# Retention and a routed expert layer: masks of whole chunks behind the routing's steps, the guess one place on, the second list's rows behind the list

## Chip, cores and metric

One NeuronCore of one Trainium2 chip. The metric is the device time of one execution in microseconds (us), the median of the runs shown. TensorE is called PE (PEld for its weight loads), VectorE DVE, ScalarE ACT, GpSimd POOL, SyncE SP.

## What is computed

A decaying linear attention over 4 x 768 tokens with 8 heads of 64 features, whose output rows are then routed, each to one of 8 experts:

```python
for t in range(S):
    state = gamma * state + outer(k[t], v[t])
    y[t] = scale * q[t] @ state
x = y.transpose(0, 2, 1, 3).reshape(3072, 512)
logits = x @ w_gate + modality_bias[modality_id]
e_idx = argmax(logits)                       # one expert for each token
gate_w = softmax(logits)[e_idx]
for e in range(8):
    h = maximum(x[e_idx == e] @ w1[e], 0)    # 512 -> 1024
    out[e_idx == e] = gate_w * (h @ w2[e])   # 1024 -> 512
```

## The kernel before, in words

**Retention.** The 3072 tokens are 24 chunks of 128, six for each sequence, three chunks being a routing group. `retention` (L1097) is a generator over the chunks n. The first nine (`WHOLE`) are done as whole chunks: `whole_state` (L287) adds a chunk to the state, `whole_scores(n + 1)` (L272) makes the next chunk's scores with PE (`sc`, two PSUM banks) and masks them on DVE in two steps (L283, tile `a`), `whole_out` (L303) multiplies masked scores and state into `y`, which ACT copies to `yT`. `tokens_out` (L368) turns a chunk's `yT` into token rows and logits: PE `x` (L375), DVE `lh` and half of `xs` (L383), ACT the other half of `xs` (L397), DVE the reduction to `lg` (L404). From chunk 9 on the chunks are done in halves: `scores`, `masked` (L210, the mask at L212), `heads_out`, `grown`, driven by `quarters` (L339). `hand_over` (L325) passes the state from the one form to the other at chunk 8. `decay_v` (L1020) scales the values on POOL (`vd`, L1024), two chunks ahead.

**Places.** Each `yield` of `retention` is a place. While the whole chunks run, the loop in `everything` (L1154) goes from place to place, three for each chunk (two for chunk 6), and at each runs one step of a queue `todo` (`tick`, L1032). Later, in `run_job` (L983), a job has 16 places t = 0 to 15; every odd one runs one step of `todo`, and every third runs a stretch of retention.

**Routing.** When the three chunks of a group have their logits, `route(gr)` (L1036) appends the group's steps to `todo`: `a` (L1040: bias, maximum, exponential), `a1` (one-hot choice `eq`, `mn`, `oh`, counts `cnt`, and for listed groups `crep`), `b` (`ranks` with PE `pc` at L615 and DVE `size`, `key`, `dg`; `route_b` with PE `rk`; `gates`), `c` (`rows_out` in some groups; `early_a` with PE `pk` at L637 and DVE `gt`, `rank`, `ohs` for listed groups), `d` (`early_b`: PE `pt` at L688 and DVE `lst`). `rows_out` has POOL scatter the group's three chunks of rows to `x_dram` (L481). `wait` is an empty step. The listed groups (`EVENTS`) are 1, 2, 4, 5 and 6: each puts two full slots of 256 tokens of one expert on a list, and so starts two expert jobs; group 7 lists the rest. `guess_a` (L649) guesses from group 0's counts which expert group 1 will list (PE `totg` at L651, DVE `key_g` to `lst_g`); SP reads the guess and loads that expert's weights, `raw`, 8 x 512 KB (L774).

**From the list to the first job.** When list 1 is there, SP reads it, loads the two halves of the slot's rows, `xg` (L806), which waits for the rows of groups 0 and 1, and issues the weights' loads again under the condition that the expert is not the guessed one (L776). Six places later (`AHEAD`) the jobs start; four and three places before that the first two pieces of the weights are cut into a high and a low part (`cut`, L778: ACT `hi_e` at L780, DVE `lo_e` at L782), two places before PE transposes the rows (`xp_e`, L825). A job is 8 pieces of `first_slot` (`h_e`, L840) and two halves of `second` (`o_e`, L855), whose result ACT scales (L867) and POOL scatters to the output (L868).

**What sets the order.** PE, ACT, DVE and SP run their instructions in the order in which the program text issues them (`manual_schedule`, L1209); POOL's order is set by a scheduler that follows the text where it can. Each engine works its queue in order, so a step that waits holds all behind it on that engine.

Of the kernel before, what the change touches and what calls it, by code (L numbers as in the profile page):

```python
# [29 lines left out]
EVENTS = {1: -1, 2: 1, 4: -1, 5: 1, 6: -1}  # L30
# [9 lines left out]
WHOLE = 9  # L40
# [13 lines left out]
def kernel(  # L54
# [23 lines left out]
    def bank(name):  # L78
        return ps.tile([P, 512], F32, tag="bank", name=name)
# [65 lines left out]
    def setup_a():  # L145
        nc.vector.tensor_copy(wgt[:, :, :P], ident.unsqueeze(1).to_broadcast([P, NG, P]))
        nc.vector.memset(ones, 1.0)
        nc.vector.memset(cnt[0], 0.0)
# [44 lines left out]
    att, psc, sts, vds = {}, {}, {}, {}  # L193
    pst = {}

    def rows(i):
        return slice(i * D, (i + 1) * D)

    def feat(n, i):
        return kqs[n][:, i].rearrange("p (g t) -> p g t", g=NG)  # L200
# [9 lines left out]
    def masked(n):  # L210
        att[n] = wk.tile([P, 2, NG, D], F32, tag="a", name=f"a_{n}")
        nc.vector.tensor_tensor(  # L212
            att[n].rearrange("p u g t -> p (u g) t"),
            psc.pop(n).rearrange("p u g t -> p (u g) t"),
            half.unsqueeze(1).to_broadcast([P, H, D]), op=ALU.mult,
        )
# [41 lines left out]
    def keep_state(n, u):  # L258

        s = sts[n, u] = wk.tile([P, NG, D], F32, tag="s", name=f"s{u}_{n}", bufs=3)  # L260
        b = (n - 1 + u) // NCH
        nc.scalar.copy(s, pst.pop(b) if u and n % NCH == NCH - 1 else pst[b])  # L262
# [9 lines left out]
    def whole_scores(n):  # L272
        kt, qt = feat(n, 0), feat(n, 1)
        p = [bank(f"sc{j}_{n}").rearrange("p (g t) -> p g t", g=NG) for j in range(2)]
        for g in range(NG):
            for j in range(2):
                nc.tensor.matmul(
                    p[j][:, g], kt[rows(j), g], qt[rows(j), g], start=True, stop=True,
                    skip_group_check=True,
                )  # L280
        att[n] = me.tile([P, 2, NG, P], F32, tag=f"hi1{2 + n % 2}", name=f"a_{n}")
        for j in range(2):
            nc.vector.tensor_tensor(  # L283
                att[n][:, j], p[j], mask.unsqueeze(1).to_broadcast([P, NG, P]), op=ALU.mult
            )
# [39 lines left out]
    def hand_over(n):  # L325
        old = sts.pop((n, 0))
        b = (n - 1) // NCH
        p = pst[b] = bank(f"st_{n}")[:, : NG * D].rearrange("p (g e) -> p g e", g=NG)
        for j in range(2):
            for g in range(NG):  # L330
                nc.tensor.matmul(
                    p[rows(1 - g % 2), 2 * j + g // 2], ident[:, rows(j)], old[:, g],
                    start=(j == 0 and g < 2), stop=True, skip_group_check=True,
                )
        keep_state(n, 0)
# [272 lines left out]
    def spread(counts):  # L608
        crep = mid["crep"] = passing("crep", [P, NE, SPE], BF16)
        nc.vector.tensor_copy(crep, counts.unsqueeze(2).to_broadcast([P, NE, SPE]))  # L610

    def ranks(t, which, first=None):
        crep = mid.pop("crep")
        pc = bank(f"pc{t}")
        nc.tensor.matmul(  # L615
            pc[:NCAND, 0:1], crep.rearrange("p e i -> p (e i)"), ones[:, 0:1],
            start=True, stop=True,
        )
        size = passing("size", [NCAND, 1])
        nc.vector.tensor_scalar(size, pc[:NCAND, 0:1], off_c, 0.0, op0=ALU.subtract, op1=ALU.max)  # L620
        nc.vector.tensor_scalar(
            size, size, float(SLOT), mid["keep"], op0=ALU.min, op1=ALU.mult
        )
        key = passing("key", [NCAND, 1])
        nc.vector.scalar_tensor_tensor(
            key, size, float(P), id_c, op0=ALU.mult, op1=ALU.add if which > 0 else ALU.subtract
        )
        if first is not None:
            nc.vector.tensor_tensor(key, key, first, op=ALU.add)
        dg = passing("dg", [NCAND, NCAND])  # L630
        nc.vector.tensor_scalar(dg, ident[:NCAND, :NCAND], key, None, op0=ALU.mult)
        mid["rk"] = (t, size, key, dg)
# [387 lines left out]
    def decay_v(n):  # L1020
        vv = kvs[n][:, 1].rearrange("p (h e) -> p h e", h=H)
        by = decw if n < WHOLE else dec
        vds[n] = wk.tile([P, H, D], F32, tag="vd", name=f"vd_{n}", bufs=3)
        ins = nc.gpsimd.tensor_tensor(  # L1024
            vds[n], vv, by[:, n % NCH].unsqueeze(2).to_broadcast([P, H, D]), op=ALU.mult
        )
        vd_last[:] = [getattr(ins, "ins", ins)]


    todo = []  # L1030
# [5 lines left out]
    def route(gr):  # L1036
        last = gr == NGRP - 1
        listed = gr in EVENTS or last

        def a():  # L1040
            route_a(gr, 0)

        def a1():
            route_a(gr, 1)
            route_a(gr, 2)
            if listed:
                spread(cnt[gr + 1])

        def b():
            if listed:  # L1050
                ranks(gr, EVENTS.get(gr, 1), mid["first"] if gr == min(EVENTS) else None)
            route_b(gr)
            gates(gr)

        def rows_out():
            for i in range(GRP):
                scatter(gr, i)

        def c():
            if gr not in (4, 5, 6):  # L1060
                rows_out()
            if gr == 0:
                guess_b()
            elif gr in EVENTS:
                early_a(gr)
            elif last:
                final_a()

        def d():
            early_b(gr)  # L1070

        def wait():
            pass

        if gr == min(EVENTS):

            a()
            todo.extend([a1, b, c, d])
        elif gr == 0:
            a()  # L1080
            todo.extend([a1, guess_a, b, c])
        elif gr < 5:
            todo.extend([a, a1, b, c])
            if gr in EVENTS:
                todo.append(d)
            if gr == 4:
                todo.append(rows_out)
        else:

            todo.extend([a, a1, wait, b, wait, c])  # L1090
            if gr in EVENTS:
                todo.extend([wait, d, rows_out])
            if last:
                todo.extend([wait, final_m, wait, final_b, pad_a, wait, pad_b, wait])
                todo.extend([lambda e=e: pad_c(e) for e in range(NE)])

    def retention(modi):  # L1097
        whole_scores(0)
        decay_v(1)
        setup_a()  # L1100
        prev = None
        for n in range(NN):
            if n < WHOLE:
                if (n + 1) % NCH:
                    whole_state(n)

                load_kv(n + 7 if n < 3 else n + 3)
                listed = n == (min(EVENTS) + 1) * GRP
                if listed:

                    tokens_out(*prev)
                    route(min(EVENTS))
                if n + 1 < WHOLE:
                    whole_scores(n + 1)
                else:
                    run(scores(n + 1))
                    masked(n + 1)
                    if (n + 1) % NCH:
                        hand_over(n + 1)
                yield n  # L1120
                if prev is not None and not listed:
                    tokens_out(*prev)
                    if n % GRP == 0:
                        route(n // GRP - 1)
                if n + 1 == WHOLE:
                    run(grown(n + 1, 0))
                    keep_state(n + 1, 1)
                if not listed:
                    yield n
                prev = None  # L1130
                yT = whole_out(n)
            else:
                yT = yield from quarters(n)
                if n + 1 < NN:
                    masked(n + 1)
                load_kv(n + 3)
            if n + 2 < NN:
                decay_v(n + 2)
            load_kq(n + 8 if n < 4 else n + 4)
            if n == 0:  # L1140
                setup_b(modi)
            elif n == 1:
                list_consts()
            if prev is not None:
                tokens_out(*prev)
                if n % GRP == 0:
                    route(n // GRP - 1)
            prev = (n, yT)
            yield n
        tokens_out(*prev)  # L1150
        route(NGRP - 1)
        yield NN
# [173 lines left out]
```

## Time and profile before

| | |
|---|---|
| median of the runs shown | 431.44 us (429.03, 431.44, 433.25) |
| the profiled execution: time, span | 433.4 us, 431.5 us |
| instructions | 12024 |
| PE, PEld busy | 403.3 us (93%), 353.1 us (82%) |
| DVE, ACT, POOL busy | 249.4 us (58%), 207.6 us (48%), 103.9 us (24%) |
| granted PE clock, mean over the span | 0.978 |
| moved by DMA | 92.79 MB, mean 215 GB/s |

Times in the profile count from the start of the span. A row of the timeline has start, duration, engine, line, operation, tile written and tiles read, and in brackets how long the engine sat idle before it and what released it. A row of waits has the waiting engine and line, what it waited for, the sum in us, the number of waits and the longest. The granted clock is 1.00 at full speed.

### The profile page before, as it was taken

The numbers are of one execution on the slowest core, as the hardware profiler recorded it, in microseconds if no ns is written. First come the engines' busy times: TensorE is split into PE (matmuls) and PEld (weight loads), VectorE is DVE, ScalarE is ACT, GpSimd is POOL, SyncE is SP. The second block draws the span as 40 slices with busy tenths as digits, with TensorE's granted clock in tenths as the row PEclk, the third lists the DMA queues.
The fourth block names the chain that finished last, engine by engine and source line by source line (L and its number), as shares of the span: only waits on it lengthen the run. The fifth ranks groups of instructions, "written<-read, shape, count | busy, mean of one in ns | idle before, by whom it ended". The sixth has DMA issues, their size and how long they took to land.

```text
span 431.5 us, 12024 instructions
## 1 busy us (share of the span) xinstructions
PE 403.3 (93%) x4596; PEld 353.1 (82%) x4596; DVE 249.4 (58%) x590; ACT 207.6 (48%) x420; POOL 103.9 (24%) x130
## 2 busy tenths in 40 slices
PE   4987979899999999999999999999999999999990
PEld 3876869888988977988888988979898998869850
DVE  1766547856636666646945765967564655635400
ACT  1324245635546455546545646636464646535310
POOL 2425301413052123113500401210774101001010
PEclk9999688999999999999999999999999999999997
DMA  8999746967796954237840304842264989995000
GB/s 287 388 402 333 306 165 235 356 203 238 238 349 244 323 212 154 88 103 235 281 162 27 139 21 160 254 162 75 94 226 125 367 286 350 352 394 219 2 25 20
DMA packets 30891, 92.79 MB, mean 215 GB/s; under 512 B 5550, under 2 KB 5678, under 8 KB 30832
## 3 DMA queue, kind: packets, MB, share of 16 engines
q1 hardware_dynamic: 25360, 77.83, 52.0%
q0 software_dynamic: 5184, 13.67, 8.7%
q8 instruction: 37, 0.61, 0.6%
q10 hardware_dynamic: 288, 0.50, 0.4%
q14 instruction: 22, 0.18, 0.1%
HBM read 94.84 MB, written 17.21 MB: 260 GB/s over the span
## 4 chain that ended last, share of the span: by engine, by line
PE 66%; issue 8%; DMA 5%; DVE 3%; ACT 2%; POOL 1%; POOLq 0%; SPq 0%; ACTq 0%
PE o_e L855 25%; PE h_e L840 23%; PE x L375 4%; PE st L267 3%; PE h_s L840 3%; PE sc L267 3%; PE y L267 2%; DMA wa_u<-in_w_dram 2%; PE xp_e L825 2%; DMA wb_u<-in_w_dram 2%; DMA kv<-in_qkv_dram 1%; DVE lo_e L782 1%; ACT hi_e L780 1%; ACT xs L397 1%; POOL out_dram L868 1%
## 5 line engine op out<-in xcount | busy, mean ns | idle before, releaser
L782 DVE TENSOR_TENSOR lo_e<-raw,hi_e 128x1024 fp32r<-128x1024 f32 x80 | 100.0, 1250 | 76.5 <-ACT hi_e L780 68.6
L840 PE MATMUL h_e<-xTh,hi_e 128*128 128x256 f32 x320 | 92.0, 287 | 0.0
L840 PE MATMUL h_e<-xTl,hi_e 128*128 128x256 f32 x320 | 90.3, 282 | 0.0
L840 PE MATMUL h_e<-xTh,lo_e 128*128 128x256 f32 x320 | 90.3, 282 | 0.0
L780 ACT CAST hi_e<-raw 128x1024 fp32r<-128x1024 f32 x80 | 83.8, 1049 | 2.8 <-DMA raw<-in_w_dram 2.8
L855 PE MATMUL o_e<-hi_e,hTh 128*128 128x512 f32 x160 | 66.1, 413 | 0.0
L855 PE MATMUL o_e<-lo_e,hTh 128*128 128x512 f32 x160 | 63.1, 395 | 0.0
L855 PE MATMUL o_e<-hi_e,hTl 128*128 128x512 f32 x160 | 63.1, 394 | 0.0
L840 PEld LDWEIGHTS h_e<-xTh,hi_e 128*128 128x128 f32 x320 | 60.9, 190 | 0.7
L840 PEld LDWEIGHTS h_e<-xTh,lo_e 128*128 128x128 f32 x320 | 60.7, 190 | 0.3
L840 PEld LDWEIGHTS h_e<-xTl,hi_e 128*128 128x128 f32 x320 | 60.8, 190 | 0.0
L868 POOL DMA_INDIRECT out_dram<-o_e,xg_e x20 | 21.5, 1073 | 109.7 <-ACT o_e L867 89.5
L789 ACT ACTIVATE hTh<-h_e 128x256 fp32r<-128x256 f32 x80 | 30.7, 388 | 33.7 <-PE h_e L840 29.9
L1024 POOL TENSOR_TENSOR vd<-kv,cst 128x512 f32<-128x512 f32 x24 | 26.5, 1103 | 74.7 <-DMA kv<-in_qkv_dram 29.9
L397 ACT ACTIVATE xs<-x,cst 128x64 f32<-128x64 f32 x96 | 22.3, 315 | 45.2 <-DVE lh L383 20.4
L481 POOL DMA_INDIRECT x_dram<-xs,pos x24 | 27.6, 1152 | 65.4 <-DVE a L212 29.8
L790 DVE SCALAR_TENSOR_TENSOR hTl<-h_e,hTh 128x256 fp32r<-128x256 f32 x80 | 33.0, 419 | 16.0 <-ACT hTh L789 14.4
L855 PEld LDWEIGHTS o_e<-lo_e,hTh 128*128 128x128 f32 x160 | 30.1, 188 | 7.1
L855 PEld LDWEIGHTS o_e<-hi_e,hTh 128*128 128x128 f32 x160 | 30.1, 188 | 6.2
L855 PEld LDWEIGHTS o_e<-hi_e,hTl 128*128 128x128 f32 x160 | 30.2, 189 | 5.6
L262 ACT COPY s<-st 128x256 f32<-128x256 f32 x36 | 13.6, 378 | 40.4 <-PE y L267 16.1
L867 ACT ACTIVATE o_e<-o_e,xg_e 128x512 f32<-128x512 f32 x20 | 13.8, 690 | 39.6 <-issue 24.0
(193 smaller groups left out, 696.0 us busy)
## 6 DMA issues: line engine op xcount, KB each, us to landing
raw<-in_w_dram SPq DMA_DIRECT2D x104, 512.0 KB
kv<-in_qkv_dram SPq DMA_DIRECT2D x24, 512.0 KB
kq<-in_qkv_dram SPq DMA_DIRECT2D x23, 512.0 KB
xg_e<-x_dram SPq DMA_DIRECT2D x20, 257.0 KB
wa_u<-in_w_dram SPq DMA_DIRECT2D x8, 512.0 KB
wb_u<-in_w_dram SPq DMA_DIRECT2D x16, 256.0 KB
xg_s<-x_dram SPq DMA_DIRECT2D x4, 257.0 KB
x_dram<-xs,pos POOLq DMA_INDIRECT x24
```

Source lines behind the costliest of these rows:

```text
L267: nc.tensor.matmul(out_, l, r, start=start, stop=True, skip_group_check=True)
L375: nc.tensor.matmul(px[:, g], yT[:, 2 * u + g], wgt[:, 2 * u + g], start=(g == 0), stop=(g == 1), skip_group_check=True,)
L397: nc.scalar.activation(x[:, i], px[:, i // 2, rows(i % 2)], AF.Copy, scale=gain[:, c, 4 * u + i : 4 * u + i + 1],)
L481: ins = nc.gpsimd.indirect_dma_start(out=x_dram[:, :], out_offset=bass.IndirectOffsetOnAxis(ap=pos[:, i : i + 1], axis=0), in_=xs, in_offs ...
L780: nc.scalar.copy(hi, raws[m][i])
L782: nc.vector.tensor_tensor(lo, raws[m][i], hi.bitcast(F32), op=ALU.subtract)
L789: nc.scalar.activation(hi, src, AF.Relu)
L790: nc.vector.scalar_tensor_tensor(lo, src, 0.0, hi.bitcast(F32), op0=ALU.max, op1=ALU.subtract)
L840: nc.tensor.matmul(ph, s["w1"][f // 2][wi][:, o : o + P], s["xT"][kc // 2][a][:, kc % 2, :], start=(n == 0), stop=(n == 3 * KC - 1),)
L855: nc.tensor.matmul(po, hT[f][a][:, hh * P : (hh + 1) * P], s["w2"][f // 2][wi][:, (f % 2) * DM : (f % 2 + 1) * DM], start=(n == 0), stop=( ...
L868: ins = nc.gpsimd.indirect_dma_start(out=out[:, :], out_offset=bass.IndirectOffsetOnAxis(ap=xg.bitcast(I32)[:, DM : DM + 1], axis=0), in_= ...
L1024: ins = nc.gpsimd.tensor_tensor(vds[n], vv, by[:, n % NCH].unsqueeze(2).to_broadcast([P, H, D]), op=ALU.mult)
```

## The change

1. The masks of the whole chunks become a function of their own, `whole_masked`, called behind the place that follows the scores, so that the `todo` step of that place is ahead of the mask on DVE. The same goes for chunk 9's mask, `masked(9)`, at chunk 8. Chunk 0's stays where it was.
2. Group 0 gets an empty step between `a1` and `guess_a`: `guess_a`, `b` and `c` come one place later.
3. Groups 2 and 3 get empty steps between `a1`, `b` and `c`, and group 2 one ahead of `d`; group 2's `rows_out` leaves `c` and follows `d`.

```diff
@@ whole_scores
                     p[j][:, g], kt[rows(j), g], qt[rows(j), g], start=True, stop=True,
                     skip_group_check=True,
                 )
+        psc[n] = p
+
+    def whole_masked(n):
+        p = psc.pop(n)
         att[n] = me.tile([P, 2, NG, P], F32, tag=f"hi1{2 + n % 2}", name=f"a_{n}")
         for j in range(2):
             nc.vector.tensor_tensor(
@@ route
         def c():
-            if gr not in (4, 5, 6):
+            if gr not in EVENTS or gr == min(EVENTS):
                 rows_out()
...
         elif gr == 0:
             a()
-            todo.extend([a1, guess_a, b, c])
+            todo.extend([a1, wait, guess_a, b, c])
+        elif gr < 4:
+            todo.extend([a, a1, wait, b, wait, c])
+            if gr in EVENTS:
+                todo.extend([wait, d, rows_out])
         elif gr < 5:
             todo.extend([a, a1, b, c])
             if gr in EVENTS:
-                todo.append(d)
-            if gr == 4:
-                todo.append(rows_out)
+                todo.extend([d, rows_out])
@@ retention
         whole_scores(0)
+        whole_masked(0)
         decay_v(1)
...
                     whole_scores(n + 1)
                 else:
                     run(scores(n + 1))
-                    masked(n + 1)
                     if (n + 1) % NCH:
                         hand_over(n + 1)
+
                 yield n
+                if n + 1 < WHOLE:
+                    whole_masked(n + 1)
+                else:
+                    masked(n + 1)
                 if prev is not None and not listed:
                     tokens_out(*prev)
```

## Prediction

> **What bounds the kernel now.** I read the busy times by stretch first, then PE's waits, then each engine in order of time around them. The first view cuts the span where PE's behaviour changes (columns: stretch, length, busy time of PE, PEld, DVE, ACT and POOL, granted clock, DMA share, GB/s).
>
> ```profile
> 57.60:67.30 9.70, 6.79 (x144) 6.33 (x144) 5.57 (x11) 5.57 (x14) 1.05 (x1) 0.65 0.65 224
> 67.30:90.00 22.70, 21.00 (x325) 19.45 (x324) 19.11 (x50) 12.22 (x27) 5.94 (x8) 1.00 0.79 276
> 90.00:150.00 60.00, 59.98 (x876) 53.80 (x875) 33.54 (x72) 33.40 (x71) 15.22 (x18) 1.00 0.80 273
> 150.00:170.00 20.00, 18.89 (x278) 15.31 (x277) 13.30 (x41) 8.72 (x18) 5.84 (x5) 1.00 0.55 199
> 170.00:415.00 245.00, 244.29 (x2289) 214.36 (x2287) 146.86 (x301) 129.80 (x233) 53.20 (x59) 1.00 0.53 182
> ```
>
> From 67.3 us, where the first expert's matmuls begin, to 415 PE is busy for all but 3.5 us of 347.7 (the sum of length less busy time over the last four rows). Whatever brings that first matmul forward, or takes one of those 3.5 us away, ends up in the total. Ahead of 67.3 PE has holes; which of them matter is the question. PE's waits, up to 67.3 and then from there on:
>
> ```profile
> PE pc L615 <- DVE crep L610: 2.4, 1, 2.4
> PE st L267 <- ACT s L262: 1.8, 1, 1.8
> PE totg L651 <- DVE cnt L438: 1.7, 1, 1.7
> PE xp_e L825 <- DMA xg_e<-x_dram: 1.1, 1, 1.1
> ...
> PE pt L688 <- DVE ohs L678: 2.1, 2, 1.5
> PE pc L615 <- DVE crep L610: 0.7, 2, 0.4
> ```
>
> The last hole before the experts is the 1.8 us ahead of 61.49, and its chain runs backwards through four queues:
>
> ```profile
> SPq L806 <- DMA x_dram<-xs,pos: 2.8, 1, 2.8
> ...
> 54.31 1.92 SPq L806 DMA_DIRECT2D xg_e<-x_dram  x2
> 57.23 3.09 SPq L776 DMA_DIRECT2D raw<-in_w_dram  x8
> ...
> 53.50 0.69 DVE L212 TENSOR_TENSOR a<-sc,cst 128x512 f32<-128x512 f32 x1 [2.57 <-PE sc L267]
> 57.33 1.04 ACT L780 CAST hi_e<-raw 128x1024 fp32r<-128x1024 f32 x1 [2.79 <-DMA raw<-in_w_dram]
> 58.41 1.23 DVE L782 TENSOR_TENSOR lo_e<-raw,hi_e 128x1024 fp32r<-128x1024 f32 x1 [4.22 <-ACT hi_e L780]
> 60.24 0.93 ACT L397 ACTIVATE xs<-x,cst 128x64 f32<-128x64 f32 x4 [1.87 <-DVE lh L383]
> 61.49 0.37 PE L267 MATMUL st<-vd,kv 64*64 64x64 f32 x2 [1.84 <-ACT s L262]
> ```
>
> SP holds the first job's row loads until the rows scattered for groups 0 and 1 have landed. The conditional weight loads stand behind them on SP, the first cut (hi, lo) behind those, and behind the cut, on DVE and ACT in order, the evacuation of chunk 7, the copy of the state and PE's st. Call S the moment the scatter has landed, 54.2 to 54.3 here: st starts at S + 7.2. So what sets the start of the experts is not PE but S. The stalls at 26 and 42 us count only as far as they delay S; the half clock that follows the second (0.50 in a row below, between 48 and 50) is free, because at full clock PE would only wait longer for st.
>
> S goes back to the list of group 1:
>
> ```profile
> 27.65 0.17 DVE L438 TENSOR_TENSOR cnt<-cnt,new 128x8 bf16<-128x8 bf16 x1
> 28.09 0.17 DVE L653 SCALAR_TENSOR_TENSOR key_g<-totg,cst 128x8 f32<-128x8 f32 x1 [0.27 <-PE totg L651]
> 29.79 1.29 DVE L283 TENSOR_TENSOR a<-sc,cst 128x512 f32<-128x512 f32 x2 [0.70 <-PE sc L277]
> 34.97 1.39 DVE L283 TENSOR_TENSOR a<-sc,cst 128x512 f32<-128x512 f32 x2 [1.72 <-PE x L375]
> 38.17 1.25 PE L375 MATMUL x<-wgt,yT 128*128 128x144 f32 x8 [0.34 <-ACT yT L321]
> 40.54 1.29 DVE L283 TENSOR_TENSOR a<-sc,cst 128x512 f32<-128x512 f32 x2
> 41.74 1.02 DVE L425 SCALAR_TENSOR_TENSOR eq<-lg,iota3m 128x24 f32<-128x24 f32 x1
> 43.64 0.21 DVE L610 COPY crep<-cnt 128x96 bf16<-128x96 bf16 x1
> 44.18 0.21 DVE L620 TENSOR_SCALAR size<-pc,cnd 96x1 f32<-96x1 f32 x1 [0.33 <-PE pc L615]
> 41.68 1.04 POOL L1024 TENSOR_TENSOR vd<-kv,cst 128x512 f32<-128x512 f32 x1 [2.81 <-issue]
> 46.89 1.03 POOL L481 DMA_INDIRECT x_dram<-xs,pos  x1 [4.17 <-DVE xs L447]
> 49.51 0.99 POOL L481 DMA_INDIRECT x_dram<-xs,pos  x1 [0.30 <-issue]
> ```
>
> Here x (38.17) is chunk 5, the last of group 1; from it the routing runs on DVE to the gates, then POOL issues three scatters (first and last shown), which end at 50.50 and land some 3.7 us later.
>
> **The parts of the change, costed.**
>
> 1. *Guess one place on.* The totg matmul goes from straight behind chunk 3's output to behind the next chunk's state and scores. Those two take 1.7 us (DVE read totg at 28.09 and had the scores, for which it waited, at 29.79), so totg now comes at about 27.9, when cnt (27.65 + 0.17 = 27.82) is there: the 1.7 us stall goes. The list of the guess stays where it was (DVE reads totg at about 28.1 either way), so the guess's weight loads start no later than now. DVE can follow: between 27.82 and 34.97 it stood idle for 0.27 + 0.70 + 1.72 = 2.7 us, more than the 1.7. Chunk 5's x also has a 0.34 wait that may stay or go: x comes 1.4 to 2.0 earlier, I take **1.7**.
>
> 2. *Masks behind the steps.* In group 1 the mask of chunk 7 (a 1.20 us step, 40.54 to 41.74) goes from in front of eq to between crep and size. On the way to the gates DVE does the same work in another order, so crep and the 2.4 us PE stall at pc come 1.2 us sooner, but the gates don't: they win only the 0.33 us that size waited for pc, now covered by the mask. The 1.02 us of eq (the neighbouring small steps take 0.2) ends with POOL's vd, which started at 41.68. After the change eq runs before that vd (which follows chunk 6's output, about 3.5 us behind the start of x), but crep comes almost at that moment: crep starts 3.5 us behind x (43.64 - 38.17 less 1.20 less 0.8). So between 0.3 (crep pays instead of eq) and 1.2 us; I take **0.5**. The case of a single-input step that pays is in the trace:
>
> ```profile
> 83.93 1.09 DVE L678 TENSOR_SCALAR ohs<-ord_r,rank,full 96x2 bf16<-96x2 f32 x1
> 83.93 1.06 POOL L1024 TENSOR_TENSOR vd<-kv,cst 128x512 f32<-128x512 f32 x1
> ```
>
> The Trainium skill (SBUF — State Buffer, section "SBUF: two separate sides") says that POOL and a DVE step with two SBUF inputs, or in a two-port mode, hold one pair of ports in turn, whole instructions long. By that rule crep may pay like ohs, and the 0.5 would be 0.3; the two rows agree with the rule.
>
> So the scatters start 1.7 + 0.5 = 2.2 us earlier, with 1.7 to 3.2 as ends. They then fall wholly into the stretch where the transfers are full:
>
> ```profile
> 48.00:50.00 2.00, 2.00 (x9) 1.73 (x8) 1.93 (x8) 0.00 (x0) 1.47 (x2) 0.50 0.98 392
> 52.00:54.00 2.00, 2.00 (x63) 1.80 (x57) 0.50 (x1) 0.70 (x2) 1.04 (x1) 1.00 0.16 35
> ```
>
> Now the last scatter lands while the engines are nearly empty (share 0.16); up to 1 us of the gain may go into sharing. I take 0.3: **S comes 1.9 us earlier**, 0.7 to 3.2.
>
> 3. *Chunk 9's mask.* At chunk 8 the first place of the loop is also where the first cut is issued, so this mask (0.69 us of work, 0.6 from start to start) moves from ahead of that cut to between lo_e and lh, into the chain from S to st. Until now it lay at 53.50, where DVE then idled 4.22 us for hi_e. **0.6 lost**, 0 to 0.7. The other masks lengthen nothing: each is needed a chunk later.
>
> 4. *The second list spaced.* Group 2's steps go from places 1, 3, 5, 7 of the first job to 1, 5, 9, 13, its scatters to 15. PE lacks 22.70 - 21.00 = 1.70 us in the stretch from 67.3 to 90, which is this list's: 1.5 at pt, the longest of the two waits there, and 0.2 at pc. The stretch holds about ten places, some 2 us each, so DVE now has about 4 us for each answer where it had 2: **1.7 gained**, 0 to 1.7. The scatters stand on POOL behind the job's second output scatter and ahead of chunk 14's vd:
>
> ```profile
> 95.36 1.05 POOL L1024 TENSOR_TENSOR vd<-kv,cst 128x512 f32<-128x512 f32 x1 [10.37 <-DMA kv<-in_qkv_dram]
> ...
> 103.17 0.97 POOL L868 DMA_INDIRECT out_dram<-o_e,xg_e  x1 [4.80 <-ACT o_e L867]
> ...
> 117.44 0.20 PE sc L267 x2
> ```
>
> Three scatters at 1.3 us put that vd near 109 instead of 95.4; PE wants it in the half-chunk that opens at 117.4: 8 us of cover. The rows themselves are wanted a job later. Group 3's spacing has no list and no stall behind it: nothing.
>
> 5. *The clock.* The waits around 57.6 to 61.5 bring the granted clock to half:
>
> ```profile
> 60.00:61.00 1.00, 0.00 (x0) 0.00 (x0) 0.43 (x3) 0.76 (x4) 0.00 (x0) 0.79 0.00 0
> 67.00:68.00 1.00, 1.00 (x8) 1.00 (x8) 0.57 (x3) 0.11 (x1) 0.00 (x0) 0.80 1.02 381
> ```
>
> That is half clock from 60.58 to 67.40, of which PE works 5.9 us and loses 3.0. With PE earlier by more than S, its idle time before st grows from 2.9 to 5 or 6 us, so the half clock stays. If it began at the restart itself, 6.8 us of it would cost 3.4: 0 to **0.4 lost**; I take 0.
>
> Sum: -1.9 + 0.6 - 1.7 = **-3.0 us**, between -4.3 (-3.2 + 0.6 - 1.7) and +0.4 (-0.7 + 0.7 + 0 + 0.4). Against the profiled execution's 433.4 that is 430.4. This execution is at the slow end of the runs shown (429.03 to 433.25); on their median, 431.44, it is **428.4**. A measurement here tells about 1%, 4.3 us, from no change, so the likeliest verdict is "within 1%".
>
> **Rivals.**
>
> *All of it counts* (0.2): crep escapes the vd, the scatters land as fast as now, mask 9 finds cover: -3.2 - 1.7 = -4.9: 426.5. For it: DVE's 2.7 us of idle. Against it: mask 9 stands plainly behind the cut.
>
> *The clock stays full* (0.06): -3.0 - 3.0, 425.4. The rows speak against it: 1.09 and 1.84 us of waiting, split by transposes, were enough to halve it. The Trainium skill (TensorE: Matmul & The Clock Gate, section "What's actually happening") has the clock halve after an idle window of about 3.4 us, free-running; read strictly, PE's transposes could break the new idle time below that. The trace differs: the clock halved at 60.58 with no idle stretch above 1.84.
>
> *S does not move* (0.16): the scatters finish only when the weight transfers drain at about 52, whenever they are issued. Then only the list's stalls count: +0.6 - 1.7 = -1.1, 430.3. For it: the share of 0.98 up to 50.
>
> *Slower: the scatters starve* (0.08). One mechanism: the rows share 16 full engines with the guess's weights. Each us that a scatter needs to land beyond today's 3.7 moves S by one. With the last scatter ending at 48.3, twice the time (7.4) puts S at 55.7, and 1.5 + 0.6 - 1.7 = +0.4; three times puts it at 59.4: +4.1, 435.5. It decides from about 7 us on. Against it: today's first two scatters run under the same load and SP waited only 2.8 us in all.
>
> **How the numbers follow.** My forecast has 0.5, the rivals 0.2, 0.06, 0.16 and 0.08. Faster by over 1% is the second and third case, 0.26; slower by over 1% the last, 0.08; within, 0.66. The range holds the sum's upper end (431.44 + 0.4) and below reaches past the best sum (427.1) into the two faster cases: 425.0 to 431.9.
>
> **What would show it.** Right: no wait at totg; pc's wait in group 1 about 1 us or less; S between 51 and 53.5; a 0.69 us mask between the first lo_e and lh; st near 60; PE still at half clock for some 6 us; no waits at pc and pt in the first job; vd of chunk 14 late and unmissed. Wrong: S unmoved, or st following something other than ACT's copy; a new PE wait at sc or y between 28 and 36 (a mask or a bank that is late); any hole in the first two jobs.

## The result and the profile after

The change ran at 429.82 us (median of 18 runs, 428.17 to 430.89), the kernel before at 432.06 us (18 runs, 429.03 to 434.26): a ratio of 0.9948, 95% interval 0.9931 to 0.9965, or 2.2 us less (1.5 to 3.0). The forecast was 428.4 us and 3.0 us less. The profiled execution took 429.9 us with a span of 428.0 and a mean granted clock of 0.979: 3.5 us less than the profiled execution of before. Ratios leave out disturbed executions, which take longer whatever the kernel; of the profiles used below only that of the early half on the third chip is of such an execution (440.9 us). The size came out nearly as predicted. The terms did not, and most of what follows is about that.

The stretches of the profile after, cut as before (stretch, length, busy time of PE, PEld, DVE, ACT and POOL, granted clock, DMA share, GB/s):

```profile
57.60:67.30 9.70, 7.26 (x150) 6.69 (x151) 6.65 (x15) 5.60 (x16) 1.42 (x1) 0.61 0.62 207
67.30:90.00 22.70, 22.70 (x374) 20.86 (x373) 17.37 (x47) 13.26 (x28) 6.06 (x8) 1.00 0.81 285
```

The second row is the list's: PE lacked 1.70 us in it and now lacks none. PE's waits show the same, and show where the early stage stands now:

```profile
PE xp_e L829 <- DMA xg_e<-x_dram: 5.2, 3, 4.1
PE pc L619 <- DVE crep L614: 1.9, 2, 1.5
```

The wait at totg is gone. The one at pc in group 1 is 1.5 instead of 2.4. But xp_e now waits 4.1 us for the rows, which took 1.1 before: what DVE and PE won ahead of 50 us they wait off again at 57. On PE, DVE and POOL around group 1, each in order of time (x is chunk 5's):

```profile
36.52 1.25 PE L379 MATMUL x<-wgt,yT 128*128 128x144 f32 x8 [0.59 <-ACT yT L325]
...
38.33 0.59 DVE L419 TENSOR_TENSOR lg<-lg,tbias 128x24 f32<-128x24 f32 x1
...
40.25 0.78 DVE L442 TENSOR_TENSOR cnt<-cnt,new 128x8 bf16<-128x8 bf16 x1
41.07 0.21 DVE L614 COPY crep<-cnt 128x96 bf16<-128x96 bf16 x1
41.20 1.28 DVE L287 TENSOR_TENSOR a<-sc,cst 128x512 f32<-128x512 f32 x2
42.39 0.20 DVE L624 TENSOR_SCALAR size<-pc,cnd 96x1 f32<-96x1 f32 x1
...
37.82 1.05 POOL L1028 TENSOR_TENSOR vd<-kv,cst 128x512 f32<-128x512 f32 x1
39.97 1.04 POOL L1028 TENSOR_TENSOR vd<-kv,cst 128x512 f32<-128x512 f32 x1 [1.10 <-PE y L319]
45.10 1.02 POOL L485 DMA_INDIRECT x_dram<-xs,pos  x1 [4.09 <-DVE full L680]
47.70 0.97 POOL L485 DMA_INDIRECT x_dram<-xs,pos  x1 [0.31 <-issue]
```

The mask stands between crep and size as planned, and the scatters start 1.8 us earlier (45.10 for 46.89). Nearly all of that is x's (36.52 for 38.17): from the start of x to the first scatter it took 8.58 us, where it took 8.72. Then SP's wait for the scattered rows, which was 2.8 us before:

```profile
SPq L810 <- DMA x_dram<-xs,pos: 5.6, 1, 5.6
```

And the chain from SP's row loads to PE's st (rows of SP, ACT, DVE and PE):

```profile
54.03 1.92 SPq L810 DMA_DIRECT2D xg_e<-x_dram  x2
56.94 3.09 SPq L780 DMA_DIRECT2D raw<-in_w_dram  x8
57.04 1.04 ACT L784 CAST hi_e<-raw 128x1024 fp32r<-128x1024 f32 x1 [6.98 <-DMA raw<-in_w_dram]
58.12 1.22 DVE L786 TENSOR_TENSOR lo_e<-raw,hi_e 128x1024 fp32r<-128x1024 f32 x1 [10.48 <-ACT hi_e L784]
59.26 0.68 DVE L212 TENSOR_TENSOR a<-sc,cst 128x512 f32<-128x512 f32 x1
59.86 0.18 DVE L387 TENSOR_TENSOR lh<-x,cst 128x32 f32<-128x32 f32 x1
...
61.80 0.37 PE L267 MATMUL st<-vd,kv 64*64 64x64 f32 x2 [1.83 <-ACT s L262]
```

The wait doubled, and the row loads went out at 54.03 instead of 54.31. S moved by 0.28 us where 1.9 were predicted. The mask of chunk 9 (59.26) stands between lo_e and lh, 0.60 us from start to start, and st comes at S + 7.77: 0.31 us **later** than before.

Yet the first h_e is earlier, 66.41 for 67.25. The half clock did it: it began at 54.9 instead of 60.6 and ended at 65.10 instead of 67.40, so the batch that starts at st had full clock sooner:

```profile
54.00:55.00 1.00, 0.00 (x0) 0.00 (x0) 0.00 (x0) 0.00 (x0) 0.96 (x1) 0.93 0.06 6
55.00:56.00 1.00, 0.00 (x0) 0.00 (x0) 0.00 (x0) 0.00 (x0) 0.00 (x0) 0.50 0.73 234
...
65.00:66.00 1.00, 1.00 (x32) 0.93 (x25) 0.74 (x2) 0.42 (x2) 0.00 (x0) 0.95 0.90 221
```

To see what became of it later, I take the ACT cast xTh that opens each later job, first in the profile of before, then in that of after:

```profile
96.30 1.08 ACT L794 CAST xTh<-xp_e 128x512 fp32r<-128x512 f32 x2 [0.21 <-PE xp_e L825]
195.61 1.08 ACT L794 CAST xTh<-xp_e 128x512 fp32r<-128x512 f32 x2 [0.21 <-PE xp_e L825]
232.28 1.05 ACT L794 CAST xTh<-xp_e 128x512 fp32r<-128x512 f32 x2
```

```profile
93.29 1.08 ACT L798 CAST xTh<-xp_e 128x512 fp32r<-128x512 f32 x2 [0.21 <-PE xp_e L829]
192.69 1.08 ACT L798 CAST xTh<-xp_e 128x512 fp32r<-128x512 f32 x2 [0.21 <-PE xp_e L829]
228.05 1.06 ACT L798 CAST xTh<-xp_e 128x512 fp32r<-128x512 f32 x2
```

The lead over before is 0.84 us at the first h_e, 3.01 at the second job, 2.92 at 193 and 4.23 at 228. So the 3.5 us of the two profiles are made of 0.84 (-0.28 of S, +0.6 of the mask, -1.15 of the clock's phase), 2.17 in the first job, 1.3 between 193 and 228, where nothing was changed, and some 0.7 given back at the end. In that last stretch the profile of before has a wait that no one foresaw, PE held by its own issuing in a burst of small matmuls; in the same batch of after there is none:

```profile
212.80 0.29 PE L267 MATMUL y<-a,vd 64*64 64x64 f32 x2 [0.29 <-issue]
...
213.56 0.27 PE L267 MATMUL st<-vd,kv 64*64 64x64 f32 x2 [0.41 <-issue]
```

### The profile page after: what moved, and what is told of

It is laid out like the page before. It is cut to its first block, busy times and chain, and to the rows that moved or that the text cites. A ratio compares the mean times of both kernels' runs of the same rounds, so it can differ in the third digit from the quotient of the medians.

```text
span 428.0 us, 12025 instructions
## 1 busy us (share of the span) xinstructions
PE 399.8 (93%) x4596; PEld 349.9 (82%) x4596; DVE 247.7 (58%) x590; ACT 207.3 (48%) x420; POOL 105.5 (25%) x130
## 3 DMA queue, kind: packets, MB, share of 16 engines
q1 hardware_dynamic: 25360, 77.83, 52.3%
## 4 chain that ended last, share of the span: by engine, by line
PE 48%; issue 20%; DMA 5%; POOL 4%; DVE 3%; ACT 3%; SPq 0%; POOLq 0%; ACTq 0%
PE o_e L859 17%; PE h_e L844 17%; PE x L379 4%; PE st L267 3%; PE sc L267 3%; POOL x_dram L545 2%; ACT hi_e L784 2%; PE y L267 2%; DVE lo_e L786 2%; DMA x_dram<-zer,pad_i 2%; POOL out_dram L872 2%; PE xp_e L829 1%; DMA kv<-in_qkv_dram 1%; DMA out_dram<-o_e,xg_e 1%; DMA wa_u<-in_w_dram 1%
## 5 line engine op out<-in xcount | busy, mean ns | idle before, releaser
L1028 POOL TENSOR_TENSOR vd<-kv,cst 128x512 f32<-128x512 f32 x24 | 27.5, 1145 | 92.7 <-DMA kv<-in_qkv_dram 36.9
L872 POOL DMA_INDIRECT out_dram<-o_e,xg_e x20 | 22.8, 1139 | 105.0 <-ACT o_e L871 84.2
L786 DVE TENSOR_TENSOR lo_s<-raw,hi_s 128x1024 fp32r<-128x1024 f32 x16 | 19.6, 1222 | 21.0 <-ACT hi_s L784 21.0
```

The lines of the kernel that those rows point to most:

```text
L786: nc.vector.tensor_tensor(lo, raws[m][i], hi.bitcast(F32), op=ALU.subtract)
L872: ins = nc.gpsimd.indirect_dma_start(out=out[:, :], out_offset=bass.IndirectOffsetOnAxis(ap=xg.bitcast(I32)[:, DM : DM + 1], axis=0), in_= ...
L1028: ins = nc.gpsimd.tensor_tensor(vds[n], vv, by[:, n % NCH].unsqueeze(2).to_broadcast([P, H, D]), op=ALU.mult)
```

## The experiments

The theory after the result: the list's spacing carries the gain; the early half (masks and guess) brings the scatters earlier, but not S, because the scattered rows move only when the guess's weight loads have left the DMA engines. The rival: the early half is worth its predicted 1.3 us, and the profile of after caught it at a bad moment.

Four chips were used. On the one of the first four kernels everything was slower and wider (the kernel before 440.21 us, 35 runs, 435.76 to 444.51), and its traces have issue waits of PE that the profile of after lacks; so for that series I rely on the traces up to the first h_e, and repeated what needed a time.

**The halves, on the wide chip.** The kernel before with the list's part of the change alone (of the diff shown: all hunks of `route` but group 0's):

```diff
-            if gr not in (4, 5, 6):
+            if gr not in EVENTS or gr == min(EVENTS):
...
+        elif gr < 4:
+            todo.extend([a, a1, wait, b, wait, c])
+            if gr in EVENTS:
+                todo.extend([wait, d, rows_out])
```

> The kernel before with group 2's and 3's steps spaced and group 2's rows behind its list, and nothing else of the change. My theory (what PE no longer waits for in the first job counts in full, the rest of the change cancels): 1.7 us less than before, ratio about 0.996, no waits at pc and pt in the first two jobs. The rival (the early stage carried the gain, the two waits are taken back later): no difference, 0.999 to 1.001.

441.01 us, ratio 1.0009 (0.9971 to 1.0047). No wait of PE is left in its first job, as it should be, but in the next one PE was held up by issuing, in a batch of 64x64 matmuls:

```profile
123.44 0.35 PE L267 MATMUL sc<-kq 64*64 64x64 f32 x4 [0.19 <-issue]
124.21 0.29 PE L267 MATMUL y<-kq,s 64*64 64x64 f32 x2 [0.42 <-issue]
124.93 0.27 PE L267 MATMUL y<-kq,s 64*64 64x64 f32 x2 [0.43 <-issue]
```

From the second job to the third it took 35.64 us (93.29 to 128.93 by the xTh casts), where after took 32.51: the 2.2 us that the list gives were taken back there. As a test of the list this run decides nothing.

The change without the spacing:

```diff
-        elif gr < 4:
-            todo.extend([a, a1, wait, b, wait, c])
-            if gr in EVENTS:
-                todo.extend([wait, d, rows_out])
         elif gr < 5:
```

> The change without the spacing: masks behind the steps and the guess one place on, group 2 and 3 as before. My theory (the landing of the scatter is what counts, it hardly moved, and chunk 9's mask costs 0.6): between -0.3 and +0.5 us, ratio 0.9995 to 1.001, with the row loads issued within 0.5 us of 54.2. The rival, the prediction's own sum for this part (-1.9 + 0.6): -1.3 us, 0.997.

Ratio 0.9967 (0.9926 to 1.0008): no change and 1.3 us both fit. Its row loads went out at 53.36 against 54.72 for the list alone on the same chip, st at 61.13 against 61.89, the first h_e at 65.97 against 66.42.

The change with chunk 9's mask back ahead of its place, and so ahead of the cut:

```diff
                     run(scores(n + 1))
+                    masked(n + 1)
...
                     whole_masked(n + 1)
-                else:
-                    masked(n + 1)
```

> The change with chunk 9's mask put back ahead of the place, so ahead of the first cut. My theory (the mask lies in the chain cut, lh, xs, state copy, st): 0.6 us less than the change, so about 2.8 us less than before, st 0.6 us nearer to the row loads (7.2 us behind their issue, not 7.8). The rival (PE waits there for something else): the time of the change.

Ratio 0.9988 (0.9947 to 1.003). The trace answers where the time can't:

```profile
53.15 1.92 SPq L810 DMA_DIRECT2D xg_e<-x_dram  x2
...
60.32 0.37 PE L267 MATMUL st<-vd,kv 64*64 64x64 f32 x2 [1.59 <-ACT s L262]
```

st is at S + 7.17, not S + 7.77: the mask behind the cut costs the 0.6 us that were predicted.

The change with half of the weights in flight: the second matrices are not loaded on the guess, but once, without a condition, behind the rows, when the list is known.

```diff
-                raw(guess, 2)
...
-                    raw(job, 2, guess)
+                    raw(job, 2)
```

> The change with the guessed expert's second matrices (four loads of 512 KB) not loaded at the guess, but without a condition behind the first job's rows. Theory A (the last scattered rows land only when the loads queued on the same 16 engines have drained, at about 52 us): the engines drain some 5 us sooner, the row loads are issued at about 52.4 (scatter end 48.7 + 3.7 as before the change) or up to 1 us sooner, 1.6 to 2.6 us less than the change. Theory B (a scatter just takes some 5 us to land): row loads still at about 54.0, the time of the change. A loss would come from chunk 11's values, whose load then stands behind 2 MB of weights.

Ratio 0.9963 (0.9927 to 0.9998). Against the kernel just told, on the same chip and with the weight loads issued at the same time (29.51 and 29.63), its last scatter ends 0.3 us earlier (48.78 and 49.08), and S is 0.9 us earlier (52.21 and 53.15), 3.4 us behind that scatter. st comes at 59.61 with the mask behind the cut still in the way. How many packets the two DMA queues moved between 46 and 48 us shows why. In this kernel (q0 is POOL's queue with the scatters, q1 that of SP's and ACT's transfers; packets, MB, share of 16 engines):

```profile
q0 software_dynamic: 80, 0.26, 34.0%
q1 hardware_dynamic: 10, 0.02, 2.6%
```

In the changed kernel, in the same two microseconds and, behind the dots, from 50 to 52:

```profile
q1 hardware_dynamic: 233, 0.85, 103.9%
...
q0 software_dynamic: 150, 0.48, 63.7%
q1 hardware_dynamic: 41, 0.13, 16.2%
```

And in the kernel before, from 50 to 52:

```profile
q0 software_dynamic: 167, 0.54, 72.4%
```

With the weights in flight the scattered rows do not move at all between 46 and 48, though the first scatter ended on POOL at 46.12. All but a few of their packets move from 49 on, in the kernel before and in the changed one alike. In six of the profiles with all the weights POOL's queue moves at most 2 packets between 46 and 48, whether the first scatter ended at 45.07 or at 47.92. (SP's queue also holds a load of 512 KB of values there, issued at 45.61 before and at 42.54 after.)

A loaded queue of SP's does not stop POOL's in every case, though. Group 0's scatters, the first of which ended at 35.15 in after, move from 38 on beside the same weights. From 38 to 39:

```profile
q1 hardware_dynamic: 73, 0.27, 68.5%
q0 software_dynamic: 32, 0.13, 32.6%
```

So the two queues can share the engines; what decides when they begin to is not shown.

**The same on a quiet chip.** The next four kernels shared a chip on which the kernel before took 431.81 us. First the change again, unedited:

> The change itself, as the measure for the other kernels of this series, since the chip of the first series ran everything slower and spread wider. Expected as measured at first: 2.2 us less than before, ratio 0.993 to 0.9965. Row loads between 53 and 54.3 us, st 7.8 us behind their issue.

428.79 us (428.18 to 429.87), ratio 0.9937 (0.991 to 0.9963). Scatters 44.04 to 47.63, S at 53.12, 5.5 us behind them; st at 60.89, S + 7.77; the first h_e at 66.40.

The list's part alone again:

> The spacing of group 2 and 3 alone once more, beside the change on one chip. My theory (the two waits in the first job count in full): 1.7 us less than before, most of what the change gives. The rival (what the first series showed on its chip: 1.4 us of new waits of PE between 90 and 150 us take it back): less than 0.5 us.

428.75 us (427.34 to 430.92), ratio 0.9933 (0.991 to 0.9956): all of the change's gain, with the waits at totg (1.7) and pc (2.4) still there. It scatters 2.2 us later than the change and lands only 0.7 later:

```profile
48.88 0.98 POOL L481 DMA_INDIRECT x_dram<-xs,pos  x1 [0.30 <-issue]
...
53.80 1.92 SPq L806 DMA_DIRECT2D xg_e<-x_dram  x2
```

With no mask behind the cut its st comes at 60.98 against the change's 60.89. On this chip the early half adds nothing to the list's.

**Opening the chain.** If S is what holds the first job, the order on SP can be turned: the conditional weight loads need only the list, not the rows. The change with the first job's row loads behind them:

```diff
-        if j is jobs[0]:
-            rows_in(s)
-        else:
-            s["at"] = [r() for r in s["at"]]
+        s["at"] = [r() for r in s["at"]]
...
                     raw(job, 2, guess)
+                    rows_in(job)
```

> The change with the first job's conditional weight loads issued ahead of its row loads on SP. My theory of the start of the experts (st waits for the cut, the cut for the conditional loads, these on SP for the scattered rows): the cut runs at about 50 us instead of 57, chunk 9's mask costs nothing any more, and what is left is the rows, whose transposes stand ahead of st on PE: st at about 59 instead of 61.8, some 2.6 us less than the change. The rival (PE's own order is the bound there): the time of the change.

426.76 us (426.09 to 427.29), ratio 0.9881 (0.9842 to 0.9921): 2.0 us less than the change. The cut no longer waits for S:

```profile
50.54 3.11 SPq L780 DMA_DIRECT2D raw<-in_w_dram  x8
53.93 0.91 SPq L810 DMA_DIRECT2D xg_e<-x_dram  x2
...
63.36 0.37 PE L844 MATMUL h_e<-xTh,hi_e 128*128 128x256 f32 x1
```

The row loads go out no earlier than in after, and the first h_e comes 3.0 us earlier than in the change on the same chip. So the chain that the prediction read, from S through the cut to st, was the right one.

With both (chunk 9's mask back, second matrices behind the rows, conditional loads first):

```diff
-                raw(guess, 2)
...
-                    raw(job, 2, guess)
+                    rows_in(job)
+                    raw(job, 2)
```

> The same, with chunk 9's mask ahead of the cut, and with the guessed expert's second matrices loaded without condition behind the rows instead of at the guess. If the landing of the scattered rows is what counts once the cut is out of the way, and if it hangs on the weights in flight: row loads at 52.3 (as with the second matrices later in the first series) instead of 54.0, so 1.5 us less than the kernel before in this list and about 4 us less than the change. If the landing does not hang on them: the time of the kernel before in this list.

423.93 us (423.09 to 424.38), ratio 0.981 (0.977 to 0.9849), the first h_e at 61.33: 2.8 us less than the kernel before in this list and 4.9 less than the change. The row loads went out at 52.49, close to the 52.3 that was expected, but that is luck. In this kernel and in the one before SP shows no wait for the scattered rows any more; the row loads stand behind the issuing of the conditional loads, which ends at 53.65 for eight of them (50.54 + 3.11) and here, with four, at 52.30 (50.23 + 2.07). So this run does not test what the landing hangs on.

**Is the early half worth anything?** Alone again, on a third chip (the kernel before 435.29 us, 432.53 to 444.98):

> The early half of the change alone again (masks behind the steps, guess one place on; the second list as before), on another chip than the first time. Theory: the gates and the scatters come some 2 us earlier, but the last rows land only when the guess's weights have drained, so S moves by 0.3 to 0.8 us and the mask of chunk 9 behind the cut takes 0.6 back: within 0.5 us of the kernel before, ratio 0.999 to 1.001, st at S + 7.8, and the stretch 68 to 90 still lacks 1.7 us of PE. Rival (the early half carries its predicted 1.3 us): ratio 0.997 or lower.

Ratio 0.9973 (0.9937 to 1.001), S at 53.53. It holds the theory's 0.999 and the rival's 0.997 alike, and with the first run's 0.9967 it leans to a gain of about 1 us.

Then the fastest version without it, that is with the masks and the guess of the kernel before:

> As cond_first_w2_later (second list spaced, the first job's conditional weights ahead of its rows on SP, the guess's second matrices behind them), but with the masks and the guess of the kernel before. Theory (the early half bought nothing because S did not follow the scatters): with S off the chain and fewer weights in flight the early half counts at last, so without it this kernel is slower than cond_first_w2_later's 0.981 by 1 to 2 us, ratio 0.984 to 0.986; the waits at totg (1.7) and pc (2.4) are back. Rival (the early half is worth nothing in any order): 0.981, within 0.5 us.

Ratio 0.9913 (0.9879 to 0.9947), slower than expected. But this chip showed the issue waits again (35.23 us from the second job to the third), so the pair was run once more, both on a fourth chip (the kernel before 431.77 us):

> The kernel of cond_first_w2_later again, now on one chip with the same kernel without the early half. Theory (with the conditional weights first on SP the list itself is the start of the chain, and the early half brings the list): 0.98 to 0.985; the first h_e near 61.5 and 3 us or so ahead of that of the other kernel. Rival (the two differed by their chips): the two ratios within 0.003 of each other.

> The kernel of cond_first_w2_later_without_early again, on one chip with the one above. Theory: 0.99 to 0.993, some 0.7% (3 us) above the kernel with the early half; the list near 51.5 and the conditional weights near 54.5. Rival: within 0.003 of it.

With the early half 423.25 us, 0.9811 (0.9786 to 0.9836); without it 425.92 us, 0.9869 (0.9846 to 0.9891). The kernel without it came out faster than I had written (0.99 to 0.993), but the 2.7 us between the two are there, and they lie where the theory has them. With the early half (the list on DVE, the conditional loads on SP, the first h_e):

```profile
46.39 0.14 DVE L696 TENSOR_TENSOR lst<-pt,base_e 1x6 int32<-1x6 f32 x1
48.97 2.07 SPq L780 DMA_DIRECT2D raw<-in_w_dram  x4
58.55 0.38 PE L844 MATMUL h_e<-xTh,hi_e 128*128 128x256 f32 x1
```

Without it:

```profile
49.30 0.14 DVE L692 TENSOR_TENSOR lst<-pt,base_e 1x6 int32<-1x6 f32 x1
51.90 2.07 SPq L776 DMA_DIRECT2D raw<-in_w_dram  x4
61.59 0.37 PE L840 MATMUL h_e<-xTh,hi_e 128*128 128x256 f32 x1
```

The list, the loads and the first h_e are all 2.9 to 3.0 us apart, and neither kernel falls to half clock between 54 and 68. Of the 2.9 us that the early half gains at the list 2.7 reach the end once nothing behind the list waits for S. Both kernels were ahead of the marks that I had written (the first h_e at 58.55, not 61.5; without the early half the list at 49.30, not 51.5). The profile of the same kernel on the quiet chip has its list 0.95 us later (47.34) and a granted clock of 0.50 from 56 to 58; the rest of the difference is not explained.

## Why the prediction was right, and where its sum was wrong

The time was right, the likeliest verdict (within 1%) too. By its steps:

**S 1.9 us earlier: this is the step that failed.** Of the 2.2 us ahead of the scatters 1.8 were there in the profile shown. What was wrong above all is the 0.3 us given for "sharing" behind them: S came 0.28 us earlier, so 1.55 of the 1.83 at the last scatter were lost. I had read the full engines at 48 to 50 as a load that slows a scatter a little. Between 46 and 48 it held the rows back altogether. In the nine profiles with this order on SP, S follows the guess's weight loads:

| kernel | weight loads issued | last scatter ends | S | behind the loads | behind the scatter |
|---|---|---|---|---|---|
| before | 30.12 | 50.50 | 54.31 | 24.2 | 3.8 |
| after | 30.62 | 48.67 | 54.03 | 23.4 | 5.4 |
| change, quiet chip | 29.57 | 47.63 | 53.12 | 23.6 | 5.5 |
| list alone, wide chip | 30.66 | 51.54 | 54.72 | 24.1 | 3.2 |
| list alone, quiet chip | 30.55 | 49.86 | 53.80 | 23.3 | 3.9 |
| early half, wide chip | 30.56 | 50.16 | 53.36 | 22.8 | 3.2 |
| early half, third chip | 29.69 | 48.95 | 53.53 | 23.8 | 4.6 |
| mask 9 back | 29.63 | 49.08 | 53.15 | 23.5 | 4.1 |
| half the weights | 29.51 | 48.78 | 52.21 | 22.7 | 3.4 |

With all the weights loaded, S lies 22.8 to 24.2 us behind their issue, and 3.2 to 5.5 behind the last scatter: an earlier scatter mostly waits longer. The pair of the wide chip is the exception: its last scatters end at 50.16 and 51.54, and S is 3.2 behind either. With half the weights the rows landed 3.4 behind a scatter that was as early as in after, where they took 5.4. This was the rival "S does not move", given 0.16; for this term it came close in two of the three pairs that follow. In the three pairs on which the early half can be read (after against before, change against list alone, early half against list alone) S moved by 0.28, 0.68 and 1.36 us. These marks count from the start of the span, and the weight loads themselves went out 0.50 later, 0.98 earlier and 0.10 earlier; counted from them S gained 0.78, -0.30 and 1.26, and the last scatter 2.33, 1.25 and 1.28. So in the quiet pair S gained nothing, and in the wide pair it followed the scatters. The time of that rival, 430.3, was not reached all the same, because two other terms came out better.

**Chunk 9's mask, 0.6 lost: right**, by S + 7.77 with it and S + 7.17 without. S and the mask together leave st where it was: +0.31, -0.09 and -0.76 us in the same three pairs.

**Guess one place on: right in the profile shown.** x of chunk 5 starts at 36.52, 1.65 earlier (1.7 predicted), and the wait at totg is gone. Counted from the weight loads it is 2.15, and 1.14 in the quiet pair (37.57 to 35.45, less 0.98), so the size is known to about half a us only.

**Masks behind the steps: too high.** From the start of x to the first scatter the change took 0.14 us less (8.58 for 8.72), where 0.5 was predicted and 0.3 was the low end; in the quiet pair it is 0.11, in the wide one 0.09. I had one step pay for POOL's vd after the change as before it. In the profile shown two did: lg (0.59, where before it took 0.18) for the vd at 37.82, and cnt (0.78 for 0.17) for the vd at 39.97. That is 1.02 us more, where eq had paid some 0.84, and it takes back over half of the 0.33 won at pc.

**Second list, 1.7 gained: right, and low.** The waits are gone, and from the first h_e to the second job after took 26.88 us against 29.05: 2.17, above the range of 0 to 1.7. The waits are 1.70 of it; where the rest comes from is not shown. Alone on a quiet chip it gave the whole gain. One step of it failed without harm: I had three scatters ahead of chunk 14's vd on POOL. POOL's order had them earlier:

```profile
83.06 1.65 POOL L485 DMA_INDIRECT x_dram<-xs,pos  x1 [3.31 <-DVE hTl L794]
...
94.51 1.05 POOL L1028 TENSOR_TENSOR vd<-kv,cst 128x512 f32<-128x512 f32 x1 [7.09 <-DMA kv<-in_qkv_dram]
```

The vd came at 94.51, not near 109.

**Clock, 0: the half clock stayed, as predicted, but was not free of change.** From st to the first h_e the nine profiles took 4.5 to 5.8 us, with and without the early half; before stood at the slow end (5.76), after at the fast one (4.61). That difference of 1.15 us hid the missing S in the profile of after.

**Not in the sum:** the issue wait near 213, 1.3 us in the profile of before. All seven profiles with the spaced list on the quiet chips and in the result took 35.4 us between those two casts, all others 36.6 to 36.7, among them every one from the wide chips. Whether the spacing removes it or the chip does is open: no profile without the spacing was taken on a chip known to be quiet, but for that of before.

So the time was right partly by luck: the list carried it, and two terms that were in no part of the sum, the clock's phase and the issue wait, made up for S and for the masks in the two profiles. The account of the list rests on the kernel with the list alone, the failure of S on the queue's packets and on the kernel with half the weights. What lets the scattered rows through beside a load, as in group 0, stays open.

## What to carry to other kernels

Before an issue is moved earlier, look at what its transfer meets: if the engines are full with a long load until T, the landing can be set by T, and the step is then worth only what lies behind T. Then follow the chain backwards one step further and ask whether what waits needs that transfer at all; here a queue's order had put loads that needed only the list behind rows that needed the landing, and turning it gave 2.0 us, and gave the early half its 2.7 back. A gain that one profile shows at a late mark should be split at marks on the way, since the phase of the clock alone moved one mark here by 1.2 us.

## What the runs showed of the hardware

**A full hardware queue can hold back the software queue's writes.** Between 46 and 48 us SP's queue moved 233 packets and POOL's none, though a scatter had been issued; with SP's queue nearly empty (10 packets) POOL's moved 80. Between 38 and 39 both moved, 73 and 32 packets. The Trainium skill (DMA: Bandwidth & Descriptors, section "Queues, rings and completion order") has each DMA engine serve the queues that have work in turn, a packet at a time. By that rule the scatter would have had a share from 46 on; the trace differs there, with none beside 233, and agrees from 38 to 39.

**PE can be held by its own issuing.** In batches of 64x64 matmuls, some 0.06 us apart in a row, PE stood for 0.2 to 0.4 us several times with nothing to wait for that the profile shows; the stretch with the holds near 213 took 1.3 us longer, and those with the holds near 124 took 2.7 to 3.1 us longer (35.2 to 35.6 for 32.5). The first showed in the profile of before and in every one from the wide and the third chip, the second in four of the six from these two, all four with the spaced list. What holds PE there was not tried.
